# An attention and highway-layer kernel: q of batches 3 and 4 summed and scaled earlier, value casts beside the exps of k, later x copies all on ScalarE

## The chip, the cores and the metric

The kernel runs on one core of a Trainium2 chip. The metric is the device time of that core in microseconds (us), given as the median of several executions. A "profile" or "trace" below is the hardware profiler's record of one execution; the span in it is some 1.8 us shorter than the time of the same execution. Engines are written as the profile writes them: PE is TensorE's matmuls, PEld its weight loads, DVE is VectorE, ACT is ScalarE, POOL is GpSimd.

## The reference

Eight batches of linear attention are followed by a highway layer over all 4608 tokens. Cut to what matters:

```python
# q, k, v: (8 batches, 8 heads, 576 tokens, 64)
q_s = exp(q - q.max(-1)) / sum(..., -1)          # softmax over the head's 64
k_s = exp(k - k.max(2))  / sum(..., 2)           # softmax over the tokens
kv  = einsum('bhsd,bhse->bhde', k_s, v)          # 64 x 64 a head
x   = einsum('bhsd,bhde->bhse', q_s, kv)         # -> 4608 x 512
H   = max(x @ w_h, 0)
T   = sigmoid(x @ w_t + b_t)
out = T * H + (1 - T) * x                        # float32
```

## The kernel before

The work of a batch is cut into small functions. Their place in the one instruction stream is a number: `at(p, f)` files a function under place `p`, and at the end all are emitted in the order of `p`. Every engine then works through its own instructions in that order. Batch c's highway layer has the places 8c to 8c+8: four gates (a matmul group into `pt`, then the tanh on ScalarE) alternate with four carries (a matmul group into `ph`, then `dd` on VectorE) and blends (`g` on VectorE).

```python
def gate(c, ob, home=None):
    ...
    for k_ in range(4):
        mm(ps, w16["t"][:, k_, ob * P : ob * P + P], xv(k_), k_ == 0, k_ == 3)
    nc.scalar.activation(ps, ps, AF.Tanh, bias=bt2[:, ob : ob + 1], scale=0.5)
    ...
for c in range(1, B + 2):
    for ob in range(4):
        p = 8 * c + 2 * ob
        at(p, E(gate, c, ob))
        at(p + 1, E(carry, c, ob))
```

The fourth matmul of a gate reads the fourth quarter of x (`xT`). Between the gates and carries of batch b-1 stands the attention of batch b: the exps of q and k (ScalarE), the sums of q in two halves and their reciprocal (VectorE), the scaling of q by it (GpSimd), the casts of v (GpSimd), the transposes of q (`pq` on TensorE, copied to `qsT` by VectorE), the products of k and v (`psk`) and, from `qsT` and the normed product `kvn`, the rows of x (`px` for 512 tokens in two pairs, `px_l` for the last 64).

```python
def q_sums(b, a):            # VectorE: 1152 elements a half
    ...
    nc.vector.reduce_sum(qsum[b][:, :, h], eq[b][:, :, h, :], axis=AX.X)

def q_scale_p(b, n0, n1):    # GpSimd
    e, r = eq[b][:, n0:n1], qsum[b][:, n0:n1]
    nc.gpsimd.tensor_mul(e, e, r.broadcast_to(list(e.shape)))

def x_pair(b, a, even=False, home=None):
    ...                      # matmuls into t[0], t[1]
    for c in range(2):
        dst = xT[g][:, 2 * a + c, :, b2, :]
        if (c == 0) if even else (a + c < 2):
            nc.scalar.copy(dst, t[c])
        else:
            nc.vector.tensor_copy(dst, t[c])
```

So of the four x copies of a batch three were on ScalarE and the fourth on VectorE. The schedule of the attention, which the change edits:

```python
for b in range(2, B):
    p = 8 * (b - 1)
    if b > 2:
        s = p + {3: -2, 4: -4}.get(b, -5)
        at(s, E(exp_half, b, "q", 0))
        at(s + 1, E(exp_half, b, "q", 1))
        ...                  # sums, reciprocal and scaling of q: in the diff
        s = p + {3: 0, 4: 0}.get(b, -1)
        at(s, E(exp_half, b, "k", 0))
        at(s + 1, E(exp_half, b, "k", 1))
        s -= 2 if b == 4 else 0
        at(s, E(cast_v, b, 0))
        at(s + 1, E(cast_v, b, 1))
        ...
    tr, kv, x = {            # places of q_trans, kv_half, x_pair/x_left
        2: ((5, 6, 6.4), (4, 6.2), (7, 7.5, 7.6)),
        3: ((4.5, 5.5, 6), (3, 4), (6.5, 7, 7.5)),
        4: ((2, 3, 4), (4, 5), (6, 6, 7)),
    }.get(b, ((2, 3, 4), (3, 4), (5, 6, 7)))
    ...
```

The softmax here doesn't subtract the row's maximum and nothing guards it: scores larger than these inputs give would overflow.

Of the kernel before, what the change touches and what calls it, by code (L numbers as in the profile page):

```python
# [18 lines left out]
def kernel(  # L19
# [10 lines left out]
    nc = tc.nc  # L30
# [3 lines left out]
    N9 = S // 64  # L34
# [239 lines left out]
    def x_pair(b, a, even=False, home=None):  # L274
        ps, tag = home or (ps_q, "qx")
        g, b2 = b // 2, b % 2
        if a == 0 and b2 == 0:
            xT[g] = xtp.tile([P, 4, NM, 2, 64], FP16, tag="xT", name=f"xT_{g}")
        t = [
            ps.tile([P, NM, 64], FP32, tag=tag, name=f"px_{b}_{a}_{c}")  # L280
            for c in range(2)
        ]
        for x in range(2):
            for c in range(2):
                r = slice(64 * c, 64 * c + 64)
                mm(
                    t[c][64 * x : 64 * x + 64].rearrange("p n d -> p (n d)"),
                    kvn[b % 2][r, x, a, :],
                    qsT[b][r, 2 * a + x, 0:NM, :].rearrange("p n d -> p (n d)"),
                    True, True,  # L290
                )
        for c in range(2):
            dst = xT[g][:, 2 * a + c, :, b2, :]
            if (c == 0) if even else (a + c < 2):
                nc.scalar.copy(dst, t[c])  # L295
            else:
                nc.vector.tensor_copy(dst, t[c])  # L297
# [140 lines left out]
    def at(p, *fs):  # L438
        events.setdefault(p, []).extend(fs)

    E = lambda f, *a: (lambda: f(*a))
# [4 lines that stand above are left out]
# [6 lines left out]
    for g in range(B // 2):  # L452
        p = 16 * (g + 1)
# [6 lines left out]
    p = 8 * B + 8  # L460
# [16 lines left out]
    for b in range(2, B):  # L477
        p = 8 * (b - 1)
        if b > 2:
            s = p + {3: -2, 4: -4}.get(b, -5)  # L480
            at(s, E(exp_half, b, "q", 0))
            at(s + 1, E(exp_half, b, "q", 1))
            if b > 3:
                at(s + 1, E(q_sums, b, 0))
                at(s + (3.5 if b == 4 else 2), E(q_sums, b, 1), E(q_recip, b))
            else:
                at(s + 2.5, E(q_sums, b, 0))
                at(s + 3.5, E(q_sums, b, 1), E(q_recip, b))
            if b > 3:
                at(s + (3.6 if b == 4 else 2), E(q_scale_p, b, 0, 4))  # L490
                at(s + (3.7 if b == 4 else 3), E(q_scale_p, b, 4, N9))
            s = p + {3: 0, 4: 0}.get(b, -1)
            at(s, E(exp_half, b, "k", 0))
            at(s + 1, E(exp_half, b, "k", 1))
            s -= 2 if b == 4 else 0
            at(s, E(cast_v, b, 0))
            at(s + 1, E(cast_v, b, 1))
            if b == 3:
                at(p + 1.6, E(q_scale_p, b, 0, 4), E(q_scale_p, b, 4, N9))
        tr, kv, x = {  # L500
            2: ((5, 6, 6.4), (4, 6.2), (7, 7.5, 7.6)),
            3: ((4.5, 5.5, 6), (3, 4), (6.5, 7, 7.5)),
            4: ((2, 3, 4), (4, 5), (6, 6, 7)),
        }.get(b, ((2, 3, 4), (3, 4), (5, 6, 7)))
        for i in range(3):
            at(p + tr[i], E(q_trans, b, i))
        at(p + kv[0], E(kv_half, b, 0))
        at(p + kv[1], E(kv_half, b, 1), E(kv_norm, b))
        at(p + x[0], E(x_pair, b, 0))
        at(p + x[1], E(x_pair, b, 1))  # L510
        at(p + x[2], E(x_left, b))
    for b in range(4, B):
        at(8 * (b - 3), *[E(load, b, w) for w in "qkv"])

    for f in [
        E(warm_up, 20),
        E(exp_half, 0, "q", 0), E(q_sums, 0, 0),
        E(exp_half, 0, "q", 1), E(q_sums, 0, 1),
        E(q_recip, 0), E(q_scale_v, 0, 0, 4), E(q_scale_v, 0, 4, N9),
        E(exp_half, 0, "k", 0), E(cast_v, 0, 0),  # L520
        E(exp_half, 0, "k", 1), E(cast_v, 0, 1),
        E(q_trans, 0, 0), E(q_trans, 0, 1), E(warm_up, 2), E(q_trans, 0, 2),
        E(warm_up, 6),
        E(kv_half, 0, 0), E(gate_bias), E(warm_up, 2), E(kv_half, 0, 1), E(kv_norm, 0),
        *[E(cast_weight, "t", k_, (nc.vector, nc.gpsimd)[k_ % 2]) for k_ in range(4)],
        E(warm_up, 4),
        E(x_pair, 0, 0), E(warm_up, 2), E(x_pair, 0, 1), E(warm_up, 1), E(x_left, 0),
        E(exp_half, 1, "q", 0), E(q_sums_tree, 1, 0),
        E(exp_half, 1, "q", 1), E(q_sums_tree, 1, 1), E(q_recip, 1),
        E(less_one, 0), E(cast_weight, "h", 0, nc.scalar, 0.5),  # L530
        E(less_one, 1), E(cast_weight, "h", 1, nc.gpsimd, 0.5),
        E(less_one, 2), E(cast_weight, "h", 2, nc.scalar, 0.5),
        E(less_one, 3), E(cast_weight, "h", 3, nc.scalar, 0.5),
        E(q_scale_p, 1, 0, 4), E(q_scale_p, 1, 4, 8),
        E(gate, 0, 0), E(gate, 0, 1), E(gate, 0, 2, (ps_q, "qx")), E(warm_mid, 5),
        E(carry, 0, 0), E(blend, 0, 0), E(carry, 0, 1), E(exp_half, 1, "k", 0),
        E(gate, 0, 3, (ps_nat, "nat")), E(blend, 0, 1), E(carry, 0, 2),
        E(q_trans, 1, 0), E(blend, 0, 2), E(carry_products, 0, 3),
        E(exp_half, 1, "k", 1),
        *[E(cast_v_head, 1, c, (nc.scalar, nc.gpsimd, nc.gpsimd, nc.scalar)[c]) for c in range(4)],  # L540
        E(q_scale_p, 1, 8, N9),
        *[E(load, 2, w) for w in "qk"], E(load, 2, "v", [nc.sync, nc.sync]),
        *[E(load, 3, w) for w in "qkv"],
        E(q_trans, 1, 1), E(kv_half, 1, 0), E(kv_half, 1, 1), E(kv_norm, 1),
        E(q_trans, 1, 2), E(carry_diff, 0, 3), E(exp_half, 2, "q", 0),
        E(x_pair, 1, 0, True), E(x_pair, 1, 1, True, (ps_ht, "ht")),
        E(q_sums_tree, 2, 0), E(exp_half, 2, "q", 1), E(q_sums_tree, 2, 1), E(q_recip, 2),
    ]:
        f()
# [33 lines left out]
```

## Time and profile before

| | before |
|---|---|
| time, median of the first 3 executions | 136.28 us (136.11 to 136.69) |
| span in the profile | 134.5 us |
| granted TensorE clock, mean of the span | 0.997 of full speed |

How to read what follows. A **stretch** here is the time from the first gate matmul of batch c to that of batch c+1, and is called "c = 2" and so on; gate (c,0) is its first instruction. The starts of these gates are read from the trace and used as markers throughout. From c = 2 on, the lengths of the changed kernel's stretches repeated in its three profiles within 0.01 us (every other kernel was profiled once), so even a tenth of a us means something there.

The first part of the profile's page of the kernel before has the busy time of each engine, its share of the span and its instructions; the second line, from the costliest groups, has the x copies on ScalarE (line, engine, operation, tiles and shapes, count, then busy us and mean ns of one, then idle time before them and what ended it):

```profile
PE 117.1 (87%) x1427; PEld 64.7 (48%) x1427; DVE 104.7 (78%) x209; ACT 90.7 (67%) x134; POOL 71.2 (53%) x65
...
L295 ACT CAST xT<-px 128x512 f16<-128x512 f32 x23 | 12.8, 593 | 7.6 <-PE px L62 7.5
```

TensorE is busy for 87% of the span, VectorE for 78% (in c = 2 and 3 VectorE is even the busier of the two, as the prediction's first table shows). What is to be had is the time in which TensorE waits: some 17 us, a good part of it at the start and the end.

### The profile page before, as it was taken

How to read it: one execution, taken by the hardware profiler on the slowest of the kernel's cores; microseconds unless marked ns; L12 is line 12 of the kernel's file. 1: busy time of each engine (PE TensorE's matmuls, PEld its weight loads, DVE VectorE, ACT ScalarE, POOL GpSimd, SP SyncE). 2: the span in 40 equal slices, each digit the busy share in tenths (PEclk: the TensorE clock that was granted, in tenths of full speed). 3: DMA queues.
4: the chain of work that ended last, by engine and by line, in shares of the span. 5: the costliest groups of instructions: out<-in, count | busy, mean ns of one | idle time of the engine just before them, and what ended most of it. 6: DMA issues, size and time to landing. Idle time of an engine off the chain costs nothing.

```text
span 134.5 us, 3493 instructions
## 1 busy us (share of the span) xinstructions
PE 117.1 (87%) x1427; PEld 64.7 (48%) x1427; DVE 104.7 (78%) x209; ACT 90.7 (67%) x134; POOL 71.2 (53%) x65
## 2 busy tenths in 40 slices
PE   4979996897898698787797999899989999999960
PEld 1325442362354255444462664466447555589950
DVE  1386667599998798977699789988998775779880
ACT  3552284989965798569579869796974566566630
POOL 2005509960599919957834982599099632430000
PEclk9999999999999999999999999999999999999998
DMA  4999999999999999995999499992007005227874
GB/s 151 356 394 370 408 403 411 411 412 411 404 412 401 413 410 415 400 361 224 262 412 411 170 255 408 404 436 105 0 0 317 2 5 212 100 102 324 351 314 161
DMA packets 15847, 40.06 MB, mean 298 GB/s; under 512 B 724, under 2 KB 1240, under 8 KB 14808
## 3 DMA queue, kind: packets, MB, share of 16 engines
q1 hardware_dynamic: 15832, 39.85, 77.0%
q8 instruction: 11, 0.18, 0.5%
q14 instruction: 4, 0.03, 0.1%
HBM read 30.41 MB, written 9.44 MB: 296 GB/s over the span
## 4 chain that ended last, share of the span: by engine, by line
PE 46%; DVE 15%; DMA 10%; ACT 10%; POOL 8%; SPq 4%; issue 3%; DVEq 0%; ACTq 0%; POOLq 0%
PE pt L62 16%; PE ph L62 13%; DMA w32h<-in_moe_w_h_dram 10%; PE nat L62 6%; POOL eq L255 6%; PE pq L67 4%; DVE r L225 4%; DVE g L358 3%; ACT pt L332 3%; PE psk L62 3%; SPq L94 3%; DVE dd L350 3%; ACT ek L170 3%; PE px L62 3%; ACT xT L295 2%
## 5 line engine op out<-in xcount | busy, mean ns | idle before, releaser
L332 ACT ACTIVATE pt<-pt,bt 128x512 f32<-128x512 f32 (+1 forms) x40 | 24.7, 620 | 20.9 <-PE pt L62 20.9
L255 POOL TENSOR_TENSOR eq<-eq,r 128x1024 f16<-128x1024 f16 (+2 forms) x16 | 29.7, 1875 | 16.9 <-DVE r L243 11.0
L62 PE MATMUL pt<-xT,w16t 128*128 128x512 f16 x128 | 33.4, 380 | 1.8 <-DVE xT L297 0.9
L62 PE MATMUL ph<-xT,w16h 128*128 128x512 f16 x128 | 33.3, 380 | 1.4 <-ACT w16h L114 0.7
L350 DVE SCALAR_TENSOR_TENSOR dd<-xT,ph 128x512 f16<-128x512 f16 x32 | 21.9, 684 | 7.9 <-PE ph L62 7.0
L358 DVE SCALAR_TENSOR_TENSOR g<-pt,dd 128x512 f16<-128x512 f32 (+1 forms) x40 | 25.0, 627 | 2.3
L367 POOL TENSOR_TENSOR g<-g,xT 128x512 f16<-128x512 f16 x18 | 20.5, 1154 | 9.3 <-DVE g L358 9.3
L170 ACT ACTIVATE eq<-q 128x1152 f16<-128x1152 f32 x16 | 18.5, 1169 | 3.7 <-DMA q<-in_q_dram 3.7
L62 PEld LDWEIGHTS <-w16t 128*128 128x128 f16 x160 | 14.1, 98 | 14.0 <-issue 2.8
L62 PEld LDWEIGHTS <-w16h 128*128 128x128 f16 x160 | 13.7, 98 | 12.4 <-ACT w16h L114 1.4
L170 ACT ACTIVATE ek<-k 128x1152 f16<-128x1152 f32 x16 | 18.5, 1169 | 1.6 <-DMA k<-in_k_dram 1.6
L225 DVE TENSOR_REDUCE r<-eq 128x18 f32<-128x1152 f16 x12 | 16.1, 1345 | 4.0 <-ACT eq L170 4.0
L182 POOL CAST v<-v 128x1152 f16<-128x1152 f32 x12 | 13.5, 1150 | 10.1 <-DMA v<-in_v_dram 10.1
L295 ACT CAST xT<-px 128x512 f16<-128x512 f32 x23 | 12.8, 593 | 7.6 <-PE px L62 7.5
L397 ACT COPY o<-nat 128x512 f32<-128x512 f32 x28 | 16.6, 593 | 1.9 <-PE nat L62 0.9
L62 PE MATMUL nat<-ident,g 128*128 128x128 f16 x142 | 17.6, 219 | 0.2
L62 PEld LDWEIGHTS <-g 128*128 128x128 f16 x144 | 13.7, 98 | 7.8 <-issue 1.4
L67 PE MATMUL pq<-ident,eq 128*128 128x128 f16 x144 | 12.0, 219 | 4.6 <-POOL eq L255 2.9
L272 DVE COPY qsT<-pq 128x1024 f16<-128x1024 f16 (+1 forms) x24 | 13.2, 554 | 3.6 <-PE pq L67 3.3
L62 PE MATMUL warm<-wide,ident 128*128 128x512 f16 x37 | 11.9, 470 | 1.8 <-DVE wide L151 1.8
L67 PEld LDWEIGHTS <-eq 128*128 128x128 f16 x144 | 9.2, 98 | 8.7 <-POOL eq L255 4.1
L62 PE MATMUL nat<-ident,xT 128*128 128x128 f16 x56 | 9.7, 219 | 0.0
(50 smaller groups left out, 104.8 us busy)
## 6 DMA issues: line engine op xcount, KB each, us to landing
out_dram<-o SPq DMA_DIRECT2D x8, 1024.0 KB, 5.0
q<-in_q_dram SPq DMA_DIRECT2D x7, 1152.0 KB, 13.2
k<-in_k_dram SPq DMA_DIRECT2D x7, 1152.0 KB, 13.2
v<-in_v_dram SPq DMA_DIRECT2D x5, 1152.0 KB, 13.6
v<-in_v_dram SPq DMA_DIRECT2D x6, 576.0 KB, 11.6
q<-in_q_dram SPq DMA_DIRECT2D x2, 576.0 KB, 4.1
k<-in_k_dram SPq DMA_DIRECT2D x2, 576.0 KB, 7.1
w32t<-in_moe_w_t_dram SPq DMA_DIRECT2D x1, 1024.0 KB, 10.9
```

Of the source, the lines that this page charges most:

```text
L62: mm = lambda o, l, r, st, sp: nc.tensor.matmul(o, l, r, start=st, stop=sp, skip_group_check=True)
L67: nc.tensor.matmul(o, i, ident, is_transpose=True, start=True, stop=True, skip_group_check=True,)
L170: nc.scalar.activation(dst[b][:, :, 2 * a : 2 * a + 2, :], in32[which][b][:, 2 * a : 2 * a + 2].rearrange("p c n d -> p n c d"), AF.Exp,)
L182: (eng or nc.gpsimd).tensor_copy(o, i)
L225: nc.vector.reduce_sum(qsum[b][:, :, h], eq[b][:, :, h, :], axis=AX.X)
L255: nc.gpsimd.tensor_mul(e, e, r.broadcast_to(list(e.shape)))
L295: nc.scalar.copy(dst, t[c])
L332: nc.scalar.activation(ps, ps, AF.Tanh, bias=bt2[:, ob : ob + 1], scale=0.5)
L350: nc.vector.scalar_tensor_tensor(dd, xv(ob), -0.5, ps, op0=ALU.mult, op1=ALU.max)
L358: nc.vector.scalar_tensor_tensor(gv(ob), th, 1.0, dd, op0=ALU.add, op1=ALU.mult)
L367: nc.gpsimd.tensor_add(gv(ob), gv(ob), xv(ob))
L397: nc.scalar.copy(o, flat(t))
```

## The change

The intent is to let TensorE wait less in c = 2 and c = 3 by having q of batches 3 and 4 scaled earlier, and to take work from VectorE in every batch. It has five parts: (1) the exps, sums and scaling of q for batches 3 and 4 get earlier places; (2) both halves of the value casts stand together with the exps of k, which for batch 4 is two places later than before and so behind the scaling of q (for batches 5 to 7 the casts move by half a place with the exps of k); (3) the fourth x copy of batches 3 to 7 goes from VectorE to ScalarE; (4) some transposes and x pairs of batches 3 and 4 move by up to one place (batch 4's second x pair from 6 to 7, behind a carry); (5) the second cast of w_h, at the start, goes from GpSimd to ScalarE.

```diff
--- before.py
+++ after.py
@@ -291,7 +291,7 @@
                 )
         for c in range(2):
             dst = xT[g][:, 2 * a + c, :, b2, :]
-            if (c == 0) if even else (a + c < 2):
+            if (c == 0) if even else (b > 2 or a + c < 2):
                 nc.scalar.copy(dst, t[c])
             else:
                 nc.vector.tensor_copy(dst, t[c])
@@ -477,30 +477,23 @@
     for b in range(2, B):
         p = 8 * (b - 1)
         if b > 2:
-            s = p + {3: -2, 4: -4}.get(b, -5)
-            at(s, E(exp_half, b, "q", 0))
-            at(s + 1, E(exp_half, b, "q", 1))
-            if b > 3:
-                at(s + 1, E(q_sums, b, 0))
-                at(s + (3.5 if b == 4 else 2), E(q_sums, b, 1), E(q_recip, b))
-            else:
-                at(s + 2.5, E(q_sums, b, 0))
-                at(s + 3.5, E(q_sums, b, 1), E(q_recip, b))
-            if b > 3:
-                at(s + (3.6 if b == 4 else 2), E(q_scale_p, b, 0, 4))
-                at(s + (3.7 if b == 4 else 3), E(q_scale_p, b, 4, N9))
-            s = p + {3: 0, 4: 0}.get(b, -1)
-            at(s, E(exp_half, b, "k", 0))
+            e0, e1, s0, s1, sc = {
+                3: (-2.6, -1.6, -1.1, -0.1, 1),
+                4: (-5.5, -4.5, -3.7, -2.7, -2.6),
+            }.get(b, (-5, -4, -3.9, -2.9, -2.8))
+            at(p + e0, E(exp_half, b, "q", 0))
+            at(p + e1, E(exp_half, b, "q", 1))
+            at(p + s0, E(q_sums, b, 0))
+            at(p + s1, E(q_sums, b, 1), E(q_recip, b))
+            at(p + sc, E(q_scale_p, b, 0, 4), E(q_scale_p, b, 4, N9))
+            s = p + {3: 0, 4: 0}.get(b, -0.5)
+            at(s, E(exp_half, b, "k", 0), E(cast_v, b, 0))
+            at(s + 0.9, E(cast_v, b, 1))
             at(s + 1, E(exp_half, b, "k", 1))
-            s -= 2 if b == 4 else 0
-            at(s, E(cast_v, b, 0))
-            at(s + 1, E(cast_v, b, 1))
-            if b == 3:
-                at(p + 1.6, E(q_scale_p, b, 0, 4), E(q_scale_p, b, 4, N9))
         tr, kv, x = {
             2: ((5, 6, 6.4), (4, 6.2), (7, 7.5, 7.6)),
-            3: ((4.5, 5.5, 6), (3, 4), (6.5, 7, 7.5)),
-            4: ((2, 3, 4), (4, 5), (6, 6, 7)),
+            3: ((4, 5, 5), (3, 4), (6, 7, 7)),
+            4: ((2, 3, 4), (4, 5), (6, 7, 7)),
         }.get(b, ((2, 3, 4), (3, 4), (5, 6, 7)))
         for i in range(3):
             at(p + tr[i], E(q_trans, b, i))
@@ -527,10 +520,7 @@
         E(x_pair, 0, 0), E(warm_up, 2), E(x_pair, 0, 1), E(warm_up, 1), E(x_left, 0),
         E(exp_half, 1, "q", 0), E(q_sums_tree, 1, 0),
         E(exp_half, 1, "q", 1), E(q_sums_tree, 1, 1), E(q_recip, 1),
-        E(less_one, 0), E(cast_weight, "h", 0, nc.scalar, 0.5),
-        E(less_one, 1), E(cast_weight, "h", 1, nc.gpsimd, 0.5),
-        E(less_one, 2), E(cast_weight, "h", 2, nc.scalar, 0.5),
-        E(less_one, 3), E(cast_weight, "h", 3, nc.scalar, 0.5),
+        *[f for k_ in range(4) for f in (E(less_one, k_), E(cast_weight, "h", k_, nc.scalar, 0.5))],
         E(q_scale_p, 1, 0, 4), E(q_scale_p, 1, 4, 8),
         E(gate, 0, 0), E(gate, 0, 1), E(gate, 0, 2, (ps_q, "qx")), E(warm_mid, 5),
         E(carry, 0, 0), E(blend, 0, 0), E(carry, 0, 1), E(exp_half, 1, "k", 0),
```

## The prediction

> **What bounds the kernel now.** The median is 136.28 us and the profiled span 134.5 us; I carry a saving in the span over to the median. I read first the busy time of each engine in stretches of one batch. A stretch runs from the first gate matmul (`pt`) of batch c to that of batch c+1; rows are c = 2 to 6; columns are busy us (instruction count) of PE, PEld, DVE, ACT, POOL, then clock, DMA share and GB/s.
>
> ```profile
> 45.70:59.20 13.50, 11.83 (x161) 6.20 (x158) 12.10 (x22) 10.48 (x16) 10.42 (x8) 1.00 1.04 409
> 59.20:73.70 14.50, 11.99 (x166) 6.37 (x164) 12.30 (x24) 10.87 (x16) 7.85 (x5) 1.00 0.89 322
> 73.70:85.30 11.60, 11.60 (x168) 6.52 (x162) 9.93 (x20) 9.94 (x16) 7.25 (x6) 1.00 0.84 294
> 85.30:97.50 12.20, 11.77 (x166) 6.54 (x162) 11.14 (x22) 10.19 (x16) 8.60 (x6) 1.00 0.54 218
> 97.50:109.70 12.20, 11.77 (x167) 6.52 (x165) 10.03 (x22) 7.99 (x13) 9.75 (x7) 1.00 0.21 88
> ```
>
> TensorE's work for one batch is about 11.6 us (row c = 4, where it never stops). So c = 2 loses 13.5 - 11.6 = 1.9 us, c = 3 loses 14.5 - 11.6 = 2.9, c = 5 and 6 lose 0.6 each: about 6 us at most, before c = 1. After 109.7 us TensorE runs almost without a gap until the tail, which the change leaves alone.
>
> What holds TensorE is in the chain of waits (start us, us, what):
>
> ```profile
> 50.45 4.20 POOL eq L255 x2
> 54.70 0.62 PE pq L67 x8
> ...
> 61.50 4.20 POOL eq L255 x2
> 65.75 0.62 PE pq L67 x8
> ...
> 94.08 1.26 DVE r L225
> 95.35 0.59 DVE dd L350
> 95.94 1.27 DVE r L225
> 97.23 0.38 DVE r L243
> 97.61 0.55 DVE g L358
> 98.16 0.61 DVE xT L297
> 98.80 0.38 PE pt L62
> ```
>
> Twice, for batches 3 and 4, the transposes `pq` wait for GpSimd's scaling of q (`eq`), 4.2 us in two instructions, which starts only when VectorE has the reciprocals of the sums (50.28 and 61.33 in the timeline). The last lines are another thing: in batch 5 (and alike in batch 4, at 81.85) VectorE's two sums, reciprocal, blend and x copy stand in line, and the fourth gate matmul of the next batch waits for that copy. The wait summary has both, and shows how often ScalarE waits for TensorE:
>
> ```profile
> ACT pt L332 <- PE pt L62: 20.9, 21, 2.2
> POOL eq L255 <- DVE r L243: 11.0, 3, 4.0
> PE pq L67 <- POOL eq L255: 2.9, 4, 0.8
> PE pt L62 <- DVE xT L297: 0.9, 2, 0.4
> ```
>
> Last, the landings of the loads (semaphore updates in the trace): q3 at 38.9, k3 41.7, v3 44.6, q4 47.5, k4 50.4, v4 53.2 us. The DMA engines are full (about 410 GB/s) until 58 us, so nothing of batch 3 or 4 can start before these.
>
> **What the Trainium skill says.** (1) "VectorE: DVE Perf Modes", the perf-mode tier table: `tensor_reduce` has only the 1x mode, so fp16 does not speed it up. The trace agrees: 1344 ns for 1152 elements. Two of them and a reciprocal (378 ns) are 3 us of VectorE per batch wherever they stand. (2) "ScalarE: Activation LUTs", What ACT_TABLE_LOAD costs: 186 ns + 0.833 ns an element with immediate operands, 612 ns for 512; the trace has 591 for the x copy on ScalarE, 684 on VectorE. (3) "GPSIMD Engine Reference", 3.1: about 2.6 cycles an element for two inputs. The trace is a little better: 4.2 us for 2304 elements is 2.2 cycles at 1.2 GHz; I use 4.2. (4) "Perfetto Trace Analysis", Optimizing Scalar/DVE Operations: where VectorE is saturated, work may go to ScalarE. VectorE's 12.10 of 13.50 and 12.30 of 14.50 us agree that it is the fuller one.
>
> **The change, part by part.**
>
> *Weight casts.* The second w_h cast moves from GpSimd (1.58 us) to ScalarE (0.6). GpSimd then has only four subtractions, paced by the weight landings (19.8 to 21.7), and ScalarE's last cast ends at about 22.9 instead of 24.2. That is 1.3 us on the chain, but it meets q2, which lands only at 30.28; its exp (to 31.46) stands before batch 1's x copies on ScalarE in both orders. VectorE's share of those copies comes earlier, so I keep 0.1 to 0.4 us.
>
> *Batch 3's sums.* Exp of q3 goes before the tanh of gate (1,3), where ScalarE idled from 39.0 to 40.56; q3 landed at 38.9, so it fits by 0.1 us. The first sum then fills 42.9 to 44.2 on VectorE and delays the `dd` of carry (1,3) by 0.85; the second ends at 47.4, the reciprocal at 47.8 instead of 50.28. GpSimd is free of its adds and value casts at 47.5, so the scaling is 47.85 to 52.05 instead of 50.45 to 54.65: 2.5 us earlier, and the two `pq` waits (0.42 + 0.81 us) go.
>
> *Batch 4's sums.* Now VectorE carries them in c = 2, where it was already full: (sum 1.28, `dd` 0.6, `qsT`) puts the second `qsT` copy at 55.2 to 55.9, and the first x pair waits about 0.9 us for it. Placing the instructions in their new order with the trace's durations, gate (3,0) starts at 58.3 instead of 59.2: **0.9 us** of the possible 1.9. But the reciprocal of batch 4 is ready at 57.8 instead of 61.33, so the scaling ends at 62.0 instead of 65.7.
>
> *Value casts of batch 4* now stand behind that scaling on GpSimd: 62.0 to 64.25. `psk` needs them at 64.6. It fits with about 0.4 us, 1.5 for the first half.
>
> *c = 3* then has no wait for `pq` (0.84 + 0.81 us before) nor for the x pair (0.86, now behind a carry): I place gate (4,0) at 70.2 instead of 73.68, so c = 3 takes 11.9 instead of 14.5: **2.6 us**.
>
> *x copies on ScalarE.* Five copies (batches 3 to 7) leave VectorE: 5 x 0.68; ScalarE gets 5 x 0.59. For c = 5 and 6 the copy follows its sibling on ScalarE (ends about 97.9 instead of 98.7), before the fourth gate matmul would want it (about 98.2): the two gaps of 0.43 go, **0.8 us**. ScalarE's load rises to about 10.2 + 0.6 = 10.8 of 11.7 us.
>
> Sum: 0.9 + 2.6 + 0.8 = 4.3, and 0.2 at the start; less 0.4 for waits of 0.05 us that my placement leaves out. **4.1 us: 136.3 - 4.1 = 132.2 us**, 3% faster.
>
> **The rivals.**
> *A. VectorE takes the wait over.* With two batches' sums inside c = 1 and c = 2, `dd` and blends come later, and PSUM banks with them: the blend of (1,3) now ends at 48.4 instead of 46.6 and carry (2,1) reuses its bank. If each step slips 0.3 us, c = 2 gains nothing or loses; the saving falls to 2.5 to 3 us (133.5). For it: 12.1 of 13.5 us. Against: the x copy leaves, and c = 3 keeps its gain because the sums are early in any case.
> *B. ScalarE becomes the bound* with a tenth more to do (order: exp, exp, then tanh (2,2), which waits for two exps of 1.1 us; and four x copies in a row before tanh of (4,0)). For it: 10.8 of 11.7 us per batch. Against: it waits 20.9 us in total for gate matmuls. If true, c = 3 to 6 take 12 us and the saving is 3 us (133.3).
> *C. GpSimd's value casts replace the wait* in c = 3: each us by which batch 4's reciprocal is later than 58.2 would delay `psk`. Saving 3 us.
> *D. The loads pace it anyway.* Before 38.9 us surely; later, v4 at 53.2 is long there. Against: c = 3 has a DMA share of only 0.89. Loads of batch 6 are issued behind the first output, which itself comes earlier.
>
> **Range and chances.** The 0.8 us of c = 5 and 6 and some 2 us of c = 3 rest on gaps read off directly; the rest on my placement. A, B or C alone leave 133.3 to 133.5; all gaps of c = 1 to 3 filled would give about 131. So 131.0 to 133.9. Faster by 2% needs at most 133.6: 0.82. Within 2%: 0.17. Slower: 0.01, for nothing is added to TensorE.
>
> **What would show it.** Right: `pq` waits for `eq` near zero; scaling of batch 3 starting near 47.9 and of batch 4 near 58; c = 3 from 14.5 to about 12 us, c = 2 from 13.5 to about 12.6, c = 5 and 6 near 11.7; no wait of `pt` for an x copy. Wrong: c = 2 at 13.5 or more with `ph` or `px` waiting for VectorE (A); `pt` waiting for ScalarE's xT, or late tanh (B); `psk` waiting for `v` (C). An unfit start, gate (1,0) later than 32.2, would also spoil it.

## The result, and the profile after

| | before | after |
|---|---|---|
| median of 4 executions each | 136.19 us (135.93 to 136.69) | 132.05 us (131.72 to 132.26) |
| span in the profile | 134.5 us | 130.5 us |
| mean granted clock in it | 0.997 | 0.996 |

The output was correct. The ratio is 0.9689, with a 95% interval of 0.9652 to 0.9726. A ratio in this document is the mean time of one kernel's fast runs over that of the other's of the same rounds, so not quite the ratio of the medians that are quoted beside it.

The stretches of the changed kernel, c = 2 to 6, with the columns that the prediction gave for those of before (stretch, length, then busy us and count of PE, PEld, DVE, ACT, POOL, then clock, DMA share and GB/s):

```profile
45.00:57.55 12.55, 11.27 (x160) 6.33 (x157) 11.60 (x22) 10.11 (x15) 9.00 (x7) 1.00 1.04 410
57.55:69.81 12.26, 11.84 (x166) 6.65 (x163) 10.89 (x22) 10.75 (x17) 9.10 (x7) 1.00 0.98 363
69.81:81.45 11.64, 11.64 (x167) 6.55 (x163) 9.34 (x19) 10.60 (x17) 7.55 (x6) 1.00 1.00 362
81.45:93.53 12.08, 11.71 (x167) 6.65 (x163) 10.57 (x22) 10.60 (x17) 8.59 (x6) 1.00 0.56 225
93.53:105.60 12.07, 11.70 (x166) 6.64 (x162) 8.76 (x20) 8.54 (x15) 9.73 (x7) 1.00 0.22 89
```

The first two stretches are shorter, as meant; c = 4 was already full (11.64 of 11.64 us) and stays so. The last two are hardly shorter than before, although VectorE has less to do in them, and TensorE still stands for 0.37 us in each. Where the 4.0 us of the span lie, from the starts of the gates:

| gate | before, us | after, us | saved so far | by the stretch ahead of it |
|---|---|---|---|---|
| (2,0) | 45.73 | 45.01 | 0.72 | 0.72 (the start) |
| (3,0) | 59.18 | 57.55 | 1.63 | 0.91 (c = 2) |
| (4,0) | 73.68 | 69.81 | 3.87 | 2.24 (c = 3) |
| (5,0) | 85.32 | 81.45 | 3.87 | 0.00 (c = 4) |
| (6,0) | 97.55 | 93.53 | 4.02 | 0.15 (c = 5) |
| (7,0) | 109.61 | 105.61 | 4.00 | -0.02 (c = 6) |

The rest of the program takes as long as before. The wait summary of the changed kernel (engine, line, what it waited for; us in total, times, longest):

```profile
POOL eq L255 <- DVE r L243: 15.9, 6, 4.0
ACT pt L332 <- PE pt L62: 14.1, 14, 2.5
...
PE psk L62 <- POOL v L182: 0.7, 2, 0.4
...
PE px L62 <- DVE qsT L272: 0.7, 1, 0.7
```

The wait of `pq` for `eq`, 2.9 us before, is no longer in the summary. GpSimd itself waits longer for the reciprocals (15.9 us instead of 11.0), which costs something only where work behind the scaling is urgent, as the value casts in c = 5 and 6 are. ScalarE waits 14.1 us for gate matmuls instead of 20.9: it has more to do and is late only where a line below says so. Two waits are new, of `px` for `qsT` and, twice, of `psk` for the value casts. In the timeline (start, busy us, instruction, then in brackets the idle time before it and its releaser) they and the two scalings are:

```profile
47.26 4.19 POOL L255 TENSOR_TENSOR eq<-eq,r 128x1024 f16<-128x1024 f16 x2 [0.26 <-DVE r L243]
...
54.97 0.41 PE L62 MATMUL px<-qsT,kvn 64*64 64x512 f16 x4 [0.70 <-DVE qsT L272]
...
56.96 4.19 POOL L255 TENSOR_TENSOR eq<-eq,r 128x1024 f16<-128x1024 f16 x2 [3.29 <-DVE r L243]
...
57.37 0.25 PE L62 MATMUL px_l<-qsT,kvn 64*64 64x64 f16 x4 [0.58 <-ACT xT L295]
...
69.63 0.25 PE L62 MATMUL px_l<-qsT,kvn 64*64 64x64 f16 x4 [0.34 <-ACT xT L295]
```

The scalings start at 47.26 and 56.96 us, instead of 50.45 and 61.50. What TensorE loses in c = 2 are 0.70 us before the first x pair and 0.58 us before the last 64 tokens' rows; in c = 3 only the 0.34 us of the last line. The chain of waits (start, us, what) shows what stands behind the 0.70 us, and what replaced the gap in c = 5:

```profile
52.46 1.26 DVE r L225
53.72 0.60 DVE dd L350
54.32 0.61 DVE qsT L272
...
54.97 0.41 PE px L62 x4
...
83.54 2.33 POOL eq L255
85.87 1.10 POOL v L182
...
87.01 0.48 PE psk L62 x36
```

In c = 2 VectorE works off batch 4's first sum and a `dd` before it copies the second `qsT`. In c = 5 GpSimd goes straight from the scaling to the first value cast, and TensorE needs that cast. The order was the same in the kernel before:

```profile
85.55 4.19 POOL L255 TENSOR_TENSOR eq<-eq,r 128x1024 f16<-128x1024 f16 x2 [3.97 <-DVE r L243]
89.68 2.24 POOL L182 CAST v<-v 128x1152 f16<-128x1152 f32 x2
```

Counted from gate (5,0), the first cast ended 5.51 us in, before and after alike (90.83 and 86.96 us). Before, TensorE had lost 0.43 us to the x copy and came to `psk` only at 91.03, 0.20 us after the cast was done; without that loss it comes too early and waits 0.37 us.

### The profile page after: what moved, and what is told of

Read it like the earlier page. It is cut to its first block, busy times and chain, and to the rows that moved or that the text cites. A ratio compares the mean times of both kernels' runs of the same rounds, so it can differ in the third digit from the quotient of the medians.

```text
span 130.5 us, 3496 instructions
## 1 busy us (share of the span) xinstructions
PE 115.9 (89%) x1427; PEld 65.4 (50%) x1427; DVE 101.0 (77%) x204; ACT 93.0 (71%) x140; POOL 69.8 (53%) x64
## 4 chain that ended last, share of the span: by engine, by line
PE 43%; DVE 21%; DMA 11%; ACT 8%; issue 6%; POOL 5%; SPq 3%; DVEq 0%; POOLq 0%; ACTq 0%
PE pt L62 14%; PE ph L62 13%; DMA q<-in_q_dram 11%; PE nat L62 6%; DVE r L225 5%; DVE dd L350 4%; PE psk L62 4%; POOL eq L255 3%; PE pq L67 3%; DVE g L358 3%; PE px L62 2%; DVE qsT L272 2%; SPq L94 2%; ACT xT L295 2%; POOL v L182 2%
## 5 line engine op out<-in xcount | busy, mean ns | idle before, releaser
L255 POOL TENSOR_TENSOR eq<-eq,r 128x1024 f16<-128x1024 f16 (+2 forms) x16 | 29.7, 1874 | 15.9 <-DVE r L243 15.9
L332 ACT ACTIVATE pt<-pt,bt 128x512 f32<-128x512 f32 (+1 forms) x40 | 24.8, 624 | 14.1 <-PE pt L62 14.1
L62 PE MATMUL pt<-xT,w16t 128*128 128x512 f16 x128 | 32.7, 380 | 1.2 <-ACT xT L295 0.9
L62 PEld LDWEIGHTS <-w16t 128*128 128x128 f16 x160 | 14.1, 98 | 14.0 <-issue 2.7
L295 ACT CAST xT<-px 128x512 f16<-128x512 f32 x28 | 15.2, 594 | 8.2 <-PE px L62 8.2
L62 PEld LDWEIGHTS <-kvn 64*64 64x64 f16 x128 | 4.2, 104 | 11.2 <-issue 7.5
```

What stands on the lines that cost most here:

```text
L62: mm = lambda o, l, r, st, sp: nc.tensor.matmul(o, l, r, start=st, stop=sp, skip_group_check=True)
```

## The experiments

The theory after the first result: the two early scalings gave what they promised (T1); the value casts, which stand behind the scaling, took over the gap in c = 5 and 6 that the x copy used to make, so part 3 of the change shows almost nothing by itself (T2); the start gained from the weight cast or from earlier exps (T3). The rivals: that the x copies give their 0.8 us after all and something else is slower; that the start is only a shift of the load landings; that the whole saving is VectorE's lighter load.

Twelve runs were made, in three sets of four, each set on one chip and five rounds each with the kernel before (set medians of before: 136.80, 136.11 and 136.03 us). All were correct. One warning first: the changed kernel itself was in two of the sets and gave 0.9689 (0.9644 to 0.9734) and 0.9726 (0.9686 to 0.9765). Differences of under 0.4% between ratios of different sets are therefore not read. Where the profile of a run fell in the slow state (the changed kernel's of the first set, and the one with batch 3 undone), its stretches from c = 2 on were still those of fast profiles (with batch 3 undone that can be checked for c = 3 to 6 alone), and only they are used.

Lengths of the stretches, us:

| kernel | c = 2 | c = 3 | c = 4 | c = 5 | c = 6 | time, us | ratio to before |
|---|---|---|---|---|---|---|---|
| before | 13.46 | 14.49 | 11.64 | 12.23 | 12.06 | 136.80; 136.11; 136.03 | 1 |
| after | 12.54 | 12.26 | 11.64 | 12.08 | 12.08 | 132.82; 132.73 | 0.9689; 0.9726 |
| batch 4 undone | 11.92 | 14.18 | 11.64 | 12.09 | 12.08 | 133.72 | 0.9777 |
| batch 3 undone | 14.34 | 12.26 | 11.64 | 12.08 | 12.08 | 134.31 | 0.9850 |
| x copies undone | 12.54 | 12.62 | 11.64 | 12.23 | 12.06 | 132.82 | 0.9705 |
| weight cast undone | 12.54 | 12.26 | 11.64 | 12.09 | 12.08 | 132.70 | 0.9701 |
| value casts first | 12.54 | 12.26 | 11.64 | 11.64 | 11.64 | 131.50 | 0.9656 |
| batch 4's sum late | 11.92 | 12.26 | 11.64 | 12.09 | 12.08 | 131.44 | 0.9660 |
| both of these | 11.92 | 12.26 | 11.64 | 11.64 | 11.64 | 130.64 | 0.9603 |
| before + weight cast | 13.46 | 14.50 | 11.64 | 12.23 | 12.06 | 136.63 | 1.0025 |
| before + casts first | 13.45 | 14.50 | 11.64 | 12.24 | 12.06 | 136.26 | 1.0028 |
| best attempt | 11.01 | 12.50 | 11.88 | 11.64 | 11.64 | 130.62 | 0.9570 |

### The changed kernel once more, as the first set's yardstick

No edit.

> The changed kernel again, as the measure for the three partial ones beside it: about 4.1 us (3.0%) below the kernel before, span about 130.5 us; gates (2,0), (3,0), (4,0), (6,0) at 45.0, 57.5, 69.8, 93.5 us.

It took 132.82 us (0.9689). The granted clock was 0.5 for 6.83 us from about 31 us on, and c = 1 took 15.12 us. Yet c = 2 to 6 are equal to the first profile within 0.01 us. So the later stretches do not depend on the start.

### Batch 4 undone

```diff
-                4: (-5.5, -4.5, -3.7, -2.7, -2.6),
+                4: (-4, -3, -3, -0.5, -0.4),
...
-            at(s, E(exp_half, b, "k", 0), E(cast_v, b, 0))
-            at(s + 0.9, E(cast_v, b, 1))
+            at(s, E(exp_half, b, "k", 0))
+            sv = s - 2 if b == 4 else s
+            at(sv, E(cast_v, b, 0))
+            at(sv + 0.9, E(cast_v, b, 1))
```

> Exps, sums, scaling and value casts of batch 4 go back to their old places; batch 3's stay early. Theory: c = 3 gets its wait of pq for the scaling back (0.8 + 0.8 us) and c = 2 wins the 0.7 us wait of px for the qsT copy: rise of 1.3 to 2.2 us, c = 2 about 11.9 and c = 3 about 14.2 us long. Rival: VectorE's line is what paces c = 2 and 3 and the order does not matter: rise under 0.5 us.

It took 133.72 us (0.9777, 0.9745 to 0.9809). c = 3 is back at 14.18 us, 1.92 longer; c = 2 is 0.62 shorter, for batch 4's sum no longer stands ahead of `qsT` there. Together that is 1.3 us, and the times differ by some 1.2 us (0.9777 - 0.9689 = 0.0088 of 136.8). The chain of waits in it has the old wait back:

```profile
59.27 4.18 POOL eq L255 x2
...
63.50 0.62 PE pq L67 x8
```

This supports T1, at the low end of what was expected. The wait of the x pair in c = 3 stays away here, so moving that pair (part 4) removed it, and not the early sums; it was not undone alone.

### Batch 3 undone

```diff
-                3: (-2.6, -1.6, -1.1, -0.1, 1),
+                3: (-2, -1, 0.5, 1.5, 1.6),
...
-            3: ((4, 5, 5), (3, 4), (6, 7, 7)),
+            3: ((4.5, 5.5, 6), (3, 4), (6.5, 7, 7.5)),
```

> Exps, sums, scaling, transposes and x pairs of batch 3 go back to their old places; batch 4's stay early. Theory: both batches' sums now meet on VectorE in c = 2, and the transposes of batch 3 wait for the scaling again: c = 2 grows from 12.5 to about 14 us, part of which c = 3 gives back; rise of 1 to 2 us over the changed kernel (about 0.980 of the kernel before). Rival: batch 4 alone made the gain, batch 3's place does not matter: rise under 0.4 us. On the start: if the exp of q3 ahead of the tanh was what made c = 1 shorter, gate (2,0) comes 15.3 us or more after q2's landing here, as before the change (15.4), instead of 14.7.

It took 134.31 us (0.9850, 0.9819 to 0.9882), so the places of batch 3 are worth some 2 us while batch 4's are kept. c = 2 is 14.34 us, 1.8 longer than with the change and 0.9 longer than before it; c = 3 is unchanged. Part of the chain of waits in c = 2:

```profile
53.82 1.26 DVE r L225
55.08 0.60 DVE qsT L272
55.67 0.59 DVE dd L350
56.27 1.27 DVE r L225
...
57.94 0.56 DVE qsT L272
...
58.54 0.41 PE px L62 x4
```

The sums of both batches stand in c = 2 now, and VectorE holds TensorE there (busy for 13.15 of 14.34 us): the two waits of `pq` for the scaling are back (0.41 and 0.81 us), and the first x pair waits 0.91 us. So batch 3's sums going into c = 1 is what makes room for batch 4's in c = 2. The two moves do not need each other, though: undone one at a time they cost 1.80 and 1.30 us in c = 2 and 3, together 3.10 of the 3.15 that the whole change gave there. Batch 3's shortens c = 2; batch 4's gives 1.92 in c = 3 and takes back 0.62 in c = 2. Rival A of the prediction is real; it just did not come true with both moved. The start of this profile can't be read, as the clock dropped in it.

### x copies undone

```diff
-            if (c == 0) if even else (b > 2 or a + c < 2):
+            if (c == 0) if even else (a + c < 2):
```

> Only the fourth x copy of batches 3 to 7 goes back to VectorE. Theory: in steady state the copy's gap of 0.43 us was only exchanged for a wait of psk for GpSimd's value cast (0.37), so undoing brings the 0.43 back, takes the 0.37 away, and costs at most 0.1 us a batch there, plus 0.2 to 0.5 in batches 3 and 4 where VectorE is fuller: rise of 0.3 to 0.7 us in all. Rival (the prediction's own 0.8 us for batches 5 and 6 alone): rise of 0.8 us or more, with c = 5 and c = 6 each 0.4 longer than in the changed kernel.

It took 132.82 us (0.9705, 0.9668 to 0.9741) against 0.9689 on the same chip: within the noise. In the stretches the copies are worth 0.36 us in c = 3, 0.15 in c = 5 and nothing (-0.02) in c = 6. This goes against the rival that they give 0.8 us in c = 5 and 6, and against the one that VectorE's lighter load is the whole saving: these copies are all the work that the change takes from VectorE, and they give 0.49 of 4.0 us.

### Value casts first, in the changed kernel

For batches 5 to 7 both casts of v go ahead of the scaling:

```diff
-            at(s, E(exp_half, b, "k", 0), E(cast_v, b, 0))
-            at(s + 0.9, E(cast_v, b, 1))
+            at(s, E(exp_half, b, "k", 0))
+            sv = s if b < 5 else p - 3
+            at(sv, E(cast_v, b, 0))
+            at(sv + (0.9 if b < 5 else 0), E(cast_v, b, 1))
```

> Value casts of batches 5 to 7 go ahead of GpSimd's scaling of the same batch, into its idle 3.5 to 4 us. Theory: the wait of psk for the value cast (0.37 us in c = 5 and in c = 6) took the place of the x copy's gap; with it gone c = 5 and c = 6 fall from 12.08 to about 11.7 us and the time falls by 0.6 to 0.8 us. Rival: something else (ScalarE, or VectorE's line) is just behind, the periods stay at 12.0 or more and the time falls by less than 0.2 us.

c = 5 and 6 fall to 11.64 us each. The stretches from c = 5 on:

```profile
81.06:92.70 11.64, 11.64 (x167) 6.54 (x163) 10.57 (x22) 10.60 (x17) 8.65 (x6) 1.00 0.58 235
92.70:104.34 11.64, 11.64 (x167) 6.54 (x163) 8.76 (x20) 8.55 (x15) 7.61 (x5) 1.00 0.22 92
```

TensorE is busy all the time in both, as in c = 4. The time is 131.50 us (0.9656, 0.9617 to 0.9694). The 0.88 us that the stretches save are 0.65% of 136 us; the ratio fell by 0.33% against one of the two results of the changed kernel and 0.70% against the other, so the times agree but would not have shown it alone. T2 is shown by the stretches.

### Value casts first, in the kernel before

```diff
+            s1 = s + 1
+            if b > 4:
+                s = s1 = p - 3.1
             at(s, E(cast_v, b, 0))
-            at(s + 1, E(cast_v, b, 1))
+            at(s1, E(cast_v, b, 1))
```

> The kernel before with only the value casts of batches 5 to 7 ahead of GpSimd's scaling; x copies stay on VectorE. Theory: there the x copy holds TensorE and psk never waits for the cast, so it gains nothing alone: c = 5 and 6 stay at 12.2 and 12.1 us, time within 0.2 us of the kernel before. Rival (the casts pace c = 5 and 6 by themselves): both fall to about 11.7 and the time falls by 0.8 us.

It took 136.26 us (1.0028, 0.9969 to 1.0087), with c = 5 and 6 at 12.24 and 12.06 us: nothing. So in c = 5 and 6 the x copies alone give 0.13 us (the changed kernel against the one with the x copies undone), the casts alone give nothing, and both give 1.0 us (24.29 to 23.28). The two waits lie on paths that run side by side, and each hid the other.

### Batch 4's first sum late

```diff
-                4: (-5.5, -4.5, -3.7, -2.7, -2.6),
+                4: (-5.5, -4.5, -2.75, -2.7, -2.6),
```

> Batch 4's first sum goes behind batch 3's second and third qsT copy on VectorE, next to its second sum. Theory: px no longer waits 0.7 us for the copy, c = 2 falls from 12.54 to 11.5 to 11.9 us, the reciprocal comes at the same time, c = 3 keeps 12.2: the time falls by 0.4 to 0.9 us. Rival: VectorE is the bound in c = 2 whatever the order; what c = 2 wins, c = 3 loses: change under 0.2 us.

c = 2 falls by 0.62 us to 11.92 and c = 3 stays at 12.26: the 0.70 us before the x pair came from the order on VectorE, and the sum can stand behind the `qsT` copy and still be in time for the scaling. The time is 131.44 us (0.9660, 0.9630 to 0.9690).

### Both of these

> Both reorderings together. Theory: they lie in different batches and add up: 1.0 to 1.6 us below the changed kernel, about 130.8 us, 0.959 of the kernel before. Rival: one of them finds the other's wait again: under 0.8 us.

The edits add up: 11.92, 12.26, 11.64, 11.64, 11.64. The time is 130.64 us (0.9603, 0.9564 to 0.9642), 4% under before; the interval lies below both of the changed kernel, though those are from other chips.

### Weight cast undone, and the weight cast alone

```diff
-        *[f for k_ in range(4) for f in (E(less_one, k_), E(cast_weight, "h", k_, nc.scalar, 0.5))],
+        *[f for k_ in range(4) for f in (
+            E(less_one, k_), E(cast_weight, "h", k_, nc.gpsimd if k_ == 1 else nc.scalar, 0.5))],
```

> Only the second w_h cast goes back to GpSimd. Theory (from the trace after): the start gain of about 0.7 us at gate (2,0) is the weight cast's, because VectorE's x copies and the sums behind them come earlier although ScalarE waits for q3's and q2's landing; undone, gate (2,0) goes back to 45.5 to 45.8 and the time rises by 0.5 to 0.7 us. Rival: the start gain is the exp of q3 moved ahead of the tanh, and the cast is hidden behind the landing of q2 (the prediction kept only 0.1 to 0.4): rise of 0 to 0.2 us.

The other way round, in the kernel before:

```diff
-        E(less_one, 1), E(cast_weight, "h", 1, nc.gpsimd, 0.5),
+        E(less_one, 1), E(cast_weight, "h", 1, nc.scalar, 0.5),
```

> The kernel before with only the second w_h cast moved to ScalarE. In the earlier traces gate (2,0) came 15.45 us after q2's landing before the change, 14.70 to 14.76 with all of it, 15.25 with only this cast undone. Theory: the cast is worth some 0.5 us of that, batch 3's exps the rest: here about 14.9 us, and the time 0.4 to 0.6 us below the kernel before. Rival: q2's landing hides the cast when it comes alone: 15.3 us or more, time within 0.2 us of the kernel before.

In the times neither shows anything: 0.9701 (0.9663 to 0.9738) against 0.9689 with the cast undone, and 1.0025 (0.9989 to 1.0061) with it alone. In the traces there is a gain. The load of q for batch 2 (q2) lands between 29.60 and 30.45 us in the profiles with a full clock up to 46 us, and the sums of batch 2 need it, so I count from its landing to gate (2,0):

| kernel | cast on | rest of the change | q2 lands | gate (2,0) | between, us |
|---|---|---|---|---|---|
| before | GpSimd | no | 30.28 | 45.73 | 15.45 |
| before + casts first | GpSimd | no | 30.29 | 45.72 | 15.43 |
| before + weight cast | ScalarE | no | 30.45 | 45.35 | 14.90 |
| weight cast undone | GpSimd | yes | 29.60 | 44.85 | 15.25 |
| after | ScalarE | yes | 30.31 | 45.01 | 14.70 |
| after, third set | ScalarE | yes | 30.11 | 44.82 | 14.71 |
| x copies undone | ScalarE | yes | 30.16 | 44.92 | 14.76 |
| value casts first | ScalarE | yes | 29.92 | 44.63 | 14.71 |

The cast is worth 0.55 us in either company, and the rest of the change 0.2 us. So T3 holds in the traces, and the rival that the landings made the gain falls: q2 landed 0.03 us later in the profile after than in that of before. The traces also show the path. In the kernel before, VectorE works through its line from the first `dd` on, with one pause of over 0.11 us (0.36 us, for `psk`), and comes to the second half of batch 2's sums at 34.13 us, 0.46 us after ScalarE's exp of it has ended (33.67), so q2 does not pace it. With the cast on ScalarE it comes there in time and starts as soon as the exp is done (33.55 after 33.52 in the profile after).

Why the times do not show the 0.55 us is only argued. It is 0.4% of the time, which the noise can hide with the cast undone; with the cast alone the interval, from 0.9989 up, leaves it out. In some profiles the granted TensorE clock halved once before the last microseconds, for 3.41 us (in the slow one of the changed kernel for 6.83): at 31 to 33 us in four kernels with the cast on ScalarE (after in the first set, batch 3 undone, batch 4's sum late, both), at 11.3 us in two (batch 4 undone, best attempt), and in none of the three profiles with the cast on GpSimd. But five profiles with it on ScalarE had no drop at all. After it c = 1 took 13.78 us (both) or 13.97 (batch 4's sum late) against 13.0, so one drop costs at least as much as the cast saves. Two windows each of the kernel with both edits and of the kernel before, around the landing of q2:

```profile
27.80:31.20 3.40, 1.89 (x81) 1.17 (x81) 3.02 (x9) 1.55 (x3) 0.59 (x2) 1.00 1.04 411
31.20:34.60 3.40, 2.94 (x15) 0.93 (x15) 2.61 (x8) 3.00 (x5) 0.05 (x1) 0.54 1.04 406
```

```profile
27.80:31.20 3.40, 2.79 (x91) 1.97 (x92) 3.04 (x10) 2.87 (x4) 1.15 (x2) 1.00 1.04 411
31.20:34.60 3.40, 2.94 (x25) 1.06 (x21) 3.31 (x8) 3.34 (x6) 0.00 (x0) 1.00 1.04 406
```

The clock column goes from 1.00 to 0.54 in the first and stays at 1.00 in the second. TensorE is through with its earlier work sooner and then busy for only 1.89 of the 3.40 us in which q2 lands, instead of 2.79. An earlier finish makes a deeper lull ahead of a landing that does not move, and a drop after it is plausible, but not shown: with the value casts first TensorE was busy for 1.92 us in the same window, and no drop followed. The mean clocks of the fast timed runs do not settle it either. They were 0.988 with the cast alone and 0.982 with both edits, which is low beside 0.994 and 0.995 of before in their sets, but 0.995 with batch 4's sum late, where the cast is on ScalarE as well; and in the first set before and the changed kernel are alike (0.992 and 0.991). So the link is left open; an x copy ahead of q2's exp, or filler matmuls in the lull, would test it, and neither was run.

### The best attempt

All of the above is put together, with the casts first from batch 4 on, batch 4's own row of places removed (it takes those of later batches), and batch 3's last x rows moved behind the next gate:

```diff
-                4: (-5.5, -4.5, -3.7, -2.7, -2.6),
+                4: (-5.5, -4.5, -2.75, -2.7, -2.6),
...
-            at(s, E(exp_half, b, "k", 0), E(cast_v, b, 0))
-            at(s + 0.9, E(cast_v, b, 1))
+            at(s, E(exp_half, b, "k", 0))
+            sv = s if b < 4 else p - 3
+            at(sv, E(cast_v, b, 0))
+            at(sv + (0.9 if b < 4 else 0), E(cast_v, b, 1))
...
-            3: ((4, 5, 5), (3, 4), (6, 7, 7)),
-            4: ((2, 3, 4), (4, 5), (6, 7, 7)),
+            3: ((4, 5, 5), (3, 4), (6, 7, 8.2)),
```

> Both reorderings, and batch 4 in the places of the later batches (casts ahead of the scaling, psk a half step sooner, x pairs one behind a carry each), and batch 3's last x rows behind the next gate. Theory: what is left of waits in c = 2 and c = 3 is x_l and px waiting for the x copies on ScalarE; so c = 2 goes from 11.92 to 11.6 to 11.8, c = 3 from 12.26 to 11.6 to 11.8, the time to about 129.7 us (0.952 of the kernel before). Rival: VectorE's line takes over in c = 2 and 3: no more than 0.3 us below the kernel with both reorderings (0.9603).

It took 130.62 us (0.9570, 0.9530 to 0.9610). c = 2 to 4 sum to 35.39 us, 0.43 less than the 35.82 of the kernel with both edits, where 0.9 was expected: c = 2 fell by 0.91, but 0.24 each came back in c = 3 and 4, in part because batch 3's last x rows now stand in c = 3. It is the fastest kernel here, but its interval overlaps that of the kernel with both edits, and the two ran on different chips, so it is not shown to be faster than that one.

### The changed kernel in the third set

No edit; the control for the best attempt.

> The changed kernel once more, as the measure beside the last version: 0.969 of the kernel before; batches c = 2 to 6 of 12.54, 12.26, 11.64, 12.08, 12.08 us; gate (2,0) 14.7 us after q2's landing where the clock stays up.

It took 132.73 us (0.9726, 0.9686 to 0.9765), with c = 2 to 6 as in the first profile within 0.01 us. The best attempt is 1.6% below it on the same chip.

## Why the prediction was right, and where it was not

The time on record was 132.2 us, and 132.05 came out. By its own steps:

- **c = 2, 0.9 us predicted: 0.91.** The order on VectorE (sum, `dd`, `qsT`) was as placed: the second `qsT` copy ran at 54.32 to 54.93 us and the pair waited 0.70 us for it. Shown by the sum moved back alone, which gives 0.62 us of it.
- **c = 3, 2.6 us predicted: 2.24.** Both waits for `pq` and the wait of the x pair went. What the placement missed is the 0.34 us in which the last x rows (`px_l`) wait for an x copy on ScalarE, in the line at 69.63 us (c = 2 had such a wait before, of 0.34 us at 59.00); with batch 4 undone c = 3 goes back to 14.18 us, and with batch 3 undone c = 2 to 14.34.
- **Scalings near 47.85 and 57.8 to 58 us: 47.26 and 56.96.** They are earlier by 0.6 us and, for batch 4, by 0.8 to 1.0, most of which is the 0.72 us of the start.
- **x copies, 0.8 us in c = 5 and 6 predicted: 0.13.** This is the term that was mis-sized most. The step was "the two gaps of 0.43 go": the copy's wait did go, but 0.37 us of waiting for the value casts took its place. Those I had counted on the path only for batch 4 (rival C), where they did fit, and never looked at for batches 6 and 7 (whose attention runs in c = 5 and 6), where they stood behind the scaling before the change as well, 0.20 us short of holding TensorE. Following GpSimd with durations, as I did for batch 4, would have shown it: in c = 5 of the profile after, the scaling starts at 81.68 us, and 4.19 us of it and 1.10 of a cast end at 86.97, while TensorE was ready for `psk` at 86.64 (87.01 less 0.37). The experiment that puts the casts first gave the missing 0.44 us in each.
- **Start, 0.2 us predicted: 0.72 in the profile.** The argument was that ScalarE's exp of q2 paces both orders, so only 0.1 to 0.4 of the cast's 1.3 us would count. That step failed: in the kernel before, VectorE was 0.46 us behind that exp. The runs show 0.55 for the cast and 0.2 for the rest, which no run takes apart. In the timed runs the cast's share does not show; why is open.
- **0.4 us of slack deducted: 0.35** is what c = 2 and 3 together fell short of 3.5 (3.5 - 3.15). The size fits by luck: it was meant for many waits of 0.05 us, and was nearly all the one wait of `px_l`.
- **Rivals.** A came true only with batch 3 undone (c = 2 at 14.34 us). B did not: ScalarE's wait for gate matmuls fell from 20.9 to 14.1 us but stayed; the waits of `px_l` for its copies are there with the x copies undone too. C happened, but in c = 5 and 6 instead of c = 3. D did not: the DMA share in c = 3 rose from 0.89 to 0.98, with no wait for loads on TensorE's path in it.

So the total came right with the main mechanism as told, but partly by luck, since two wrong terms cancelled: 0.67 us too much in c = 5 and 6, 0.5 too little at the start.

## What to carry to other kernels

On an engine that works in order, look first at where an instruction stands, and then at how much the engine has to do: early sums paid here because a 4.2 us scaling and the transposes hung on them, and one of these sums, standing one `qsT` copy too early, cost 0.62 us. When a small gap is removed, ask which second path ends just behind it, and follow that engine with durations as well; here a copy and a cast each hid the other, and only both moves together gave 1.0 us. For changes of under 1% compare the lengths between markers inside one trace, beside the granted clock, before the medians.

## What the Trainium skill lacked or had wrong

- **"TensorE: Matmul & The Clock Gate", Part 1** (the two states, and "HAM oscillation"): it puts the halved clock down to an idle window of about 3.4 us and gives as the abstract rule no idle gaps over that. Here the drops did last 3.41 us or twice that, as its window says; but they came with no gap of TensorE over 1.6 us ahead of those at 31 to 33 us and none over 2.52 ahead of those at 11 us, after windows in which it was busy for 1.0 to 2.1 us of 3.41. No threshold of the busy time comes out of these profiles: a window with 1.69 us (batch 4's sum late, 8.50 to 11.91 us, with most of a gap of 2.07 us in it) was not followed by a drop, and one with 2.14 us was. Its later section, "A second HAM failure mode", does speak of short idle stretches that make the clock swing, but has no busy share for it.
- **"GPSIMD Engine Reference", 3.1**: about 2.6 cycles an element of two inputs; the scaling's 2304 elements took 4.18 to 4.20 us, which is 2.2 at the 1.2 GHz that the same page uses. The plain add of two tensors (`g`, 1154 ns for 512 elements) comes to 2.7 and agrees with the page, so the scaling's second input, one value repeated over 64 elements, may be the difference; no run tests that.
- **No page** tells how far the landing of a load moves from one execution to the next: q2 landed between 29.6 and 30.5 us in eight profiles at a full clock and at 31.0 in a ninth. Anything that waits for it moves along, as does the place of a lull.
